# Joining a weight's low word by two 16-bit operations in place of a 32-bit shift and an and-or

## The chip, the core and the metric

One core of one Trainium2 chip runs the whole program as one launch. The metric is the device time of that launch in microseconds (us). It is given as a median of several executions, and one execution was also taken with the hardware profiler. Five engines work from queues of their own: PE (TensorE, matmul), DVE (VectorE), ACT (ScalarE), POOL (GpSimd) and SP (SyncE), which issues most of the DMAs.

## What is computed

Attention over 8 batches of 8 heads, with 32 global rows and 512 local rows per head (a local row sees the global keys and the local keys at most 32 places away), followed by a feed-forward layer on the 4352 rows of 512 features that come out of it:

```python
x = attention(q_l, k_l, v_l, q_g, k_g, v_g)   # (8 * 544, 512)
h = x @ w_in                                  # w_in  (512, 2048)
sp = np.maximum(h, 0.0) + np.log1p(np.exp(-np.abs(h)))
g = h * erf(sp)
out = (g @ w_out).astype(np.float32)          # w_out (2048, 512)
```

The weights arrive as 64-bit floating-point numbers, since setup divides a float32 array by the square root of a NumPy scalar; the kernel gets their bit patterns as 64-bit integers and makes 32-bit numbers of them on the chip.

## The kernel before

**The two stages.** Attention runs head by head. The feed-forward layer runs over nine chunks of rows (eight of 512 and one of the 256 global rows) and in two passes, `ps` 0 and 1, each with one half of the 2048 hidden features. Attention and the first pass are interleaved until some 425 us; after that the first pass ends and the second begins, which goes on until the end. Every matrix product of the feed-forward layer is made of three matmuls on split numbers, high times high, high times low and low times high, in groups that add up in PSUM (names `h` for the first product, `op` for the second, `xh`/`xl`, `gh`/`gl`, `winh`/`winl`, `wouth`/`woutl` for the high and low parts).

**The weights.** They come in sixteen units, four of `w_in` and four of `w_out` for each pass. A unit is one tile `RAW` of 128 partitions by 1024 64-bit words (lines 884 to 930, `load_unit`); two such tiles are in use in turn. Six steps make a high and a low part of it:

- `last_bits`: the lower 32-bit word becomes its own top three bits (DVE).
- `sign`: the sign bit of the upper word is put in with them (DVE).
- `rebase`: the upper word, read as a float32, is multiplied by 2 to the power -112 (ACT or DVE).
- `whole`: the upper word is shifted left by 3 and the lower word is put in (DVE).
- a copy to the high part (ACT or DVE), and a subtraction for the low part (DVE or POOL).

All of the first four work in place. Each of them reads and writes one 32-bit word of every two, so it takes steps of 8 bytes over the 1024 numbers of a partition:

```python
def word(n):
    return RAW.ap.bitcast(I32).rearrange("p (n two) -> p n two", two=2)[:, :, n]
```

Eight units are made between 16 and 128 us (first pass) and eight between 430 and 546 us (second pass). The second pass also makes sums and differences of weight parts (`sums`, line 1016: tiles `sx`, `sy`, `s0h` to `s3l`), which lie in buffers that the weights of the first pass had (line 1019). `s3l` takes the buffer `oh2`, and so comes after the last matmul that reads `wouth` of unit 2 of the first pass.

**The order.** No engine chooses at run time. `Program.schedule` (line 147) goes through all operations with a cost for each, such as `{"DVE": 0.67}` for `last_bits` and `{"DVE": 1.16}` for `sign`, and writes one fixed order per engine; until some 54 us it also puts matmuls on a constant (tile `spare`) where PE would otherwise have nothing. The engines then run their lists in order and wait for each other by semaphores. Lines 350 to 373 hold the helpers that record every instruction, so most instructions of PE have line 350, those of ACT line 352, and those of DVE and POOL line 371.

Of the kernel before, what the change touches and what calls it, by code (L numbers as in the profile page):

```python
# [13 lines left out]
BF16 = mybir.dt.bfloat16  # L14
I32 = mybir.dt.int32
I64 = mybir.dt.int64
AF = mybir.ActivationFunctionType
ALU = mybir.AluOpType
AX = mybir.AxisListType
# [48 lines left out]
SET_EXP = "exp_and_others"  # L68
SET_SOFTPLUS = "softplus"
SET_ERF = "sigmoid_and_others"  # L70


def s32(v):
    return v - (1 << 32) if v >= 1 << 31 else v


def win_start(b):
# [22 lines left out]
class Program:  # L100
# [9 lines left out]
    def add(self, ways, key, fn, reads=(), writes=(), moved=0.0, heat=0, issues=1, fetch=0, mode=0):  # L110


        op = Op()
        op.ways, op.fn, op.key, op.seq, op.moved = ways, fn, key, len(self.ops), moved
        op.heat, op.issues, op.fetch, op.mode = heat, issues, fetch, mode
        op.outs, op.at, op.new, op.eng = [], 0.0, [], None
        op.slack = max(SLACK.get(e, 0.0) for e in ways)
        op.port = not any(b.pool in self.psum for b in reads)
        deps = set()
        for b in reads:  # L120
            deps.update(b.writers)
        for b in writes:
            deps.update(b.writers)
            deps.update(b.readers)
            if b not in self.allocated:
                self.allocated.add(b)
                if b.pool is not None:
                    op.new.append(b)
        op.bufs = [b for b in dict.fromkeys([*reads, *writes]) if b.pool is not None]
        for b in op.bufs:  # L130
            b.users += 1
        for b in writes:
            b.writers, b.readers = [op], []
        for b in reads:
            if b not in writes:
                b.readers.append(op)
        op.waits = len(deps)
        for d in deps:
            d.outs.append(op)
        self.ops.append(op)  # L140
        return op
# [170 lines left out]
def kernel(  # L312
# [43 lines left out]
    def dma(*a, **k):  # L356
        i = pinned(nc.sync.dma_start(*a, **k))
        if DEPTH <= len(issued) < FEW:
            after = mybir.DependencyInfo(mybir.DependencyClass.Sync, mybir.DependencyReason.DATA)
            tc.add_manual_dep(i.ins, issued[-DEPTH].ins.name, after, reason="few in flight")  # L360
        issued.append(i)
        return i
# [10 lines left out]
    dve, pool = Pin(nc.vector), Pin(nc.gpsimd)  # L373
    vec = {"DVE": dve, "POOL": pool}

    def copy(e, dst, src):
        if e == "ACT":
            act(dst, src, AF.Copy)
        else:
            dve.tensor_copy(dst, src)  # L380
# [38 lines left out]
    part = [dram.tile([SL, DM], F32, name=f"part{c}") for c in range(NCHT)]  # L419
# [25 lines left out]
    def attention(b, h, key):  # L445
# [68 lines left out]
        def exps(src, k):  # L514
            for t in range(4):
                act(SM.ap[:, t, :], src[:, t, :], AF.Exp, bias=MX.ap[:, t : t + 1], scale=k)

        def scaled_exps():
            act(MX.ap, MX.ap, AF.Copy, scale=-scale)
            exps(S.ap, scale)  # L520
# [10 lines left out]
        else:  # L531
# [7 lines left out]
            )  # L539
            add({"ACT": 0.55}, key, lambda: act(SM.ap, SM.ap, AF.Exp, scale=scale), [TAB], [SM])  # L540
        if b * H + h < TURN:
# [52 lines left out]
    def weighted_end(b, h, nm, key, O, XN):  # L594
# [11 lines left out]
        def norm(e):  # L606
# [4 lines left out]
            else:  # L611
                for t in range(4):
                    act(XN.ap[:, t, r0 : r0 + D], O.ap[:, t, :D], AF.Copy, scale=RS.ap[:, t, :])

# [97 lines left out]
    def half_keys(key, nm, qks, GA, GB):  # L712
# [30 lines left out]
        def exps():  # L743
            for r, T in enumerate((GA, GB)):
                src = T.ap[:, :384].rearrange("p (m x) -> p m x", x=P)
                dst = PG.ap[:, 3 * r : 3 * r + 3, :]
                for x in (slice(0, WB), slice(2 * WB, 4 * WB)):
                    act(dst[:, :, x], src[:, :, x], AF.Exp, bias=NM.ap[:, r : r + 1], scale=scale)

# [131 lines left out]
    def mbuf(shape, dtype, name, tag, bufs):  # L881
        return Buf(mp, shape, dtype, name, tag, bufs)

    def load_unit(kind, src, half, u, hi, lo, key, deps=()):
        HI, LO = (
            Buf(pool, [P, 2, 512], F32R, f"w{kind}{x}_{half}_{u}", tag)
            for x, (pool, tag) in (("h", hi), ("l", lo))
        )
        RAW = mbuf([P, 1024], I64, f"raw_{kind}_{half}_{u}", "raw", 2)

        def fetch():
            for i in range(2):
                dma(RAW.ap[:, 512 * i : 512 * i + 512], src[half, u][:, 512 * i : 512 * i + 512])

        add({"SP": 0.9}, key - RLEAD, fetch, deps, [RAW, HI, LO], moved=1048.0, issues=2)

        def word(n):
            return RAW.ap.bitcast(I32).rearrange("p (n two) -> p n two", two=2)[:, :, n]

        def last_bits():  # L900
            dve.tensor_scalar(word(0), word(0), 29, None, op0=ALU.logical_shift_right)

        def sign():
            dve.scalar_tensor_tensor(word(0), word(1), s32(0x80000000), word(0), op0=ALU.bitwise_and, op1=ALU.bitwise_or)

        def rebase(e):
            w = word(1).bitcast(F32)
            if e == "ACT":
                act(w, w, AF.Copy, scale=REBASE)
            else:  # L910
                dve.tensor_scalar(w, w, REBASE, None, op0=ALU.mult)

        def whole():
            dve.scalar_tensor_tensor(word(1), word(1), 3, word(0), op0=ALU.logical_shift_left, op1=ALU.bitwise_or)

        flat = lambda t: t.ap.rearrange("p a n -> p (a n)")
        LOW, UP = Buf(None, None, None, None, None), Buf(None, None, None, None, None)
        add({"DVE": 0.67}, key, last_bits, [RAW], [LOW])
        add({"DVE": 1.16}, key, sign, [RAW, LOW], [LOW, UP])
        add({"ACT": 1.05, "DVE": 0.67}, key, rebase, [RAW, UP], [UP])  # L920
        add({"DVE": 1.16}, key, whole, [RAW, LOW, UP], [UP])
        add({"ACT": 1.05, "DVE": 0.67}, key, lambda e: copy(e, flat(HI), word(1).bitcast(F32)), [RAW, UP], [HI])
        add(
            {"POOL": 2.45, "DVE": 1.16},
            key,
            lambda e: vec[e].tensor_tensor(flat(LO), word(1).bitcast(F32), flat(HI).bitcast(F32), ALU.subtract),
            [RAW, HI, UP],
            [LO],
        )
        W[kind, half, u] = (HI, LO)  # L930
# [363 lines left out]
    for u in range(NU):  # L1294
        load_unit("in", w_in, 0, u, (wpool, f"ih{u}"), (wpool, f"il{u}"), WIN[u])
        load_unit("out", w_out, 0, u, (wpool, f"oh{u}"), (wpool, f"ol{u}"), WOUT[u])
# [9 lines left out]
    def load_late(i):  # L1306
        kind, src, u = ("in", w_in, i) if i < NU else ("out", w_out, i - NU)
        load_unit(kind, src, 1, u, late[2 * i], late[2 * i + 1], LATE[i], [ATTN])
# [8 lines left out]
    for ps in range(2):  # L1317
        for c in ORDER[ps]:
            n = NV if c < B else NU
# [110 lines left out]
```

## Time and profile before

| | us |
|---|---|
| median of 3 executions | 904.11 |
| lowest and highest of them | 901.39, 904.65 |
| the profiled execution, its own time | 905.85 |
| the profiled execution, span from the first to the last instruction | 904.04 |
| busy in the span: PE, DVE, ACT, POOL | 891.8, 674.5, 522.2, 244.2 |

The span is 1.81 us shorter than the profiled execution's own time. [...] A busy share is an average over the whole span; the stages differ, and PE's instructions are pipelined, so a short hole between two matmuls can be read better from their starts than from the idle time that is given for them.

### The profile page before, as it was taken

Reading aid. Unit: us, or ns where it says so; the run is one execution under the profiler, and the core shown is the slowest. Engines: PE = TensorE matmul, PEld = TensorE weight load, DVE = VectorE, ACT = ScalarE, POOL = GpSimd, SP = SyncE. Lnnn points to the kernel's source line nnn. Section 1 sums busy time; section 2 is a strip of 40 time slices with the busy share of each in tenths; the row PEclk is TensorE's granted clock in tenths of the full one; section 3 lists DMA queues with packets and bytes.
Section 4 is the critical chain, followed back from the end, with each engine's and each line's share of the span. In section 5 each row is a group of like instructions: output and inputs, shape, how many; then the busy total and the mean of one; then the engine's idle time right before and its main releaser. Section 6 shows DMA issues by size and latency. Waiting matters only on the chain.

```text
span 904.0 us, 22910 instructions
## 1 busy us (share of the span) xinstructions
PE 891.8 (99%) x9289; PEld 736.2 (81%) x9300; DVE 674.5 (75%) x1567; ACT 522.2 (58%) x962; POOL 244.2 (27%) x181
## 2 busy tenths in 40 slices
PE   9999999999999999999999999999999999999998
PEld 5677777777777777778898888988999899999986
DVE  3899797667757676773985898898878787787553
ACT  4778882855557466663756664655454545453540
POOL 0002242312533115330510324354222323233100
PEclk9999999999999999999999999999999999999999
DMA  9997988889798898975452210321324152303034
GB/s 349 349 314 232 301 256 241 303 242 319 261 257 276 252 307 269 278 239 164 131 136 95 115 47 1 71 63 33 70 71 94 57 115 60 96 24 95 1 94 116
DMA packets 93209, 153.53 MB, mean 170 GB/s; under 512 B 11952, under 2 KB 55728, under 8 KB 93104
## 3 DMA queue, kind: packets, MB, share of 16 engines
q1 hardware_dynamic: 92912, 151.81, 53.9%
q8 instruction: 73, 1.20, 0.6%
q10 hardware_dynamic: 192, 0.26, 0.1%
q14 instruction: 32, 0.26, 0.1%
HBM read 111.41 MB, written 40.63 MB: 168 GB/s over the span
## 4 chain that ended last, share of the span: by engine, by line
PE 80%; DVE 12%; DMA 4%; issue 2%; ACT 1%; POOL 1%; SPq 0%; DVEq 0%; POOLq 0%
PE op L350 34%; PE h L350 32%; PE s L350 5%; DVE raw_in L371 2%; PE o L350 2%; PE spare L350 2%; PE ga L350 2%; DMA rx<-xsc 2%; DVE xl L371 2%; DVE hs L371 1%; PE go L350 1%; PE s L351 1%; DVE gl L371 1%; DVE xh L371 1%; DVE sp L371 1%
## 5 line engine op out<-in xcount | busy, mean ns | idle before, releaser
L350 PE MATMUL op<-wouth,gh 128*128 128x512 f32 x544 | 217.5, 400 | 0.6 <-issue 0.6
L350 PE MATMUL op<-woutl,gh 128*128 128x512 f32 x544 | 212.4, 390 | 0.0
L350 PE MATMUL op<-wouth,gl 128*128 128x512 f32 x544 | 212.1, 390 | 0.0
L371 POOL TENSOR_TENSOR sp<-sp,hs 128x512 f32<-128x512 f32 x78 | 113.0, 1471 | 271.6 <-ACT sp L352 271.6
L350 PE MATMUL h<-xh,winh 128*128 128x512 f32 (+1 forms) x464 | 164.6, 355 | 0.6 <-DVE hs L371 0.5
L350 PE MATMUL h<-xh,winl 128*128 128x512 f32 (+1 forms) x464 | 162.2, 350 | 0.0
L350 PE MATMUL h<-xl,winh 128*128 128x512 f32 (+1 forms) x464 | 162.0, 349 | 0.0
L350 PEld LDWEIGHTS op<-wouth,gh 128*128 128x128 f32 x544 | 102.2, 188 | 27.3 <-issue 6.4
L350 PEld LDWEIGHTS op<-wouth,gl 128*128 128x128 f32 x544 | 102.1, 188 | 22.2
L350 PEld LDWEIGHTS op<-woutl,gh 128*128 128x128 f32 x544 | 102.3, 188 | 19.0 <-issue 0.5
L353 ACT ACT_TABLE_LOAD x90 | 115.5, 1283 | 2.3 <-PEq L1417 0.7
L352 ACT ACTIVATE gh<-sp 128x512 fp32r<-128x512 f32 x85 | 52.0, 631 | 92.8 <-PE op L350 84.4
L371 DVE TENSOR_TENSOR gl<-sp,gh 128x512 fp32r<-128x512 f32 x105 | 96.5, 939 | 7.2 <-ACT gh L352 6.4
L350 PEld LDWEIGHTS h<-xh,winh 128*128 128x128 f32 x464 | 87.7, 189 | 17.1 <-issue 2.7
L352 ACT ACTIVATE hs<-h 128x512 f32<-128x512 f32 (+1 forms) x68 | 36.9, 543 | 110.4 <-PE h L350 110.0
L350 PEld LDWEIGHTS h<-xl,winh 128*128 128x128 f32 x464 | 87.8, 189 | 12.0
L350 PEld LDWEIGHTS h<-xh,winl 128*128 128x128 f32 x464 | 87.7, 189 | 11.7
L371 DVE TENSOR_TENSOR hs<-h,hs 128x256 f32<-128x256 f32 x196 | 76.5, 417 | 11.8 <-PE h L350 7.7
L352 ACT ACTIVATE sp<-hs 128x512 f32<-128x512 f32 x136 | 74.9, 620 | 0.7 <-DVE gl L371 0.4
L352 ACT ACTIVATE sp<-sp 128x512 f32<-128x512 f32 x136 | 74.8, 620 | 0.4
L371 POOL TENSOR_TENSOR gl<-sp,gh 128x512 fp32r<-128x512 f32 x31 | 46.4, 1505 | 80.2 <-ACT gh L352 41.9
L371 DVE CAST gh<-sp 128x512 fp32r<-128x512 f32 x51 | 32.9, 652 | 43.2 <-PE op L350 42.8
(179 smaller groups left out, 1538.9 us busy)
## 6 DMA issues: line engine op xcount, KB each, us to landing
vb<-in_vB_dram SPq DMA_DIRECT2D x32, 650.0 KB, 5.7
qk<-in_qk_dram SPq DMA_DIRECT2D x30, 656.0 KB, 7.0
rx<-xsc SPq DMA_DIRECT2D x52, 256.0 KB, 5.2
va<-in_vA_dram SPq DMA_DIRECT2D x32, 390.0 KB, 5.8
px<-tp SPq DMA_DIRECT2D x84, 128.0 KB, 4.8
pt<-px SPq DMA_DIRECT2D x21, 512.0 KB, 5.5
raw_in<-in_w_in_dram SPq DMA_DIRECT2D x16, 512.0 KB, 7.3
xsc<-xT SPq DMA_DIRECT2D x32, 256.0 KB, 5.5
```

Of the source, the lines that this page charges most:

```text
L350: pe = lambda n, *a, **k: pinned(nc.tensor.matmul(n, *a, **k))
L351: tr = lambda *a, **k: pinned(nc.tensor.transpose(*a, **k))
L352: act = lambda *a, **k: pinned(nc.scalar.activation(*a, **k))
L353: table = lambda name: pinned(nc.scalar.preload_act_table_set(name))
L371: return lambda *a, **k: pinned(f(*a, **k))
```

## The change

`sign` no longer joins two tensors. `last_bits` shifts the upper 16 bits of the lower word right by 13 and writes the result to that word's lower 16 bits. `sign` then takes the sign bit out of the upper word's top 16 bits and writes it, alone, over the lower word's upper 16 bits. Together the two halves are the word that stood there before. Both operations have one tensor as input, a constant, and 16-bit elements in steps of 8 bytes, 1024 of them per partition.

```diff
+U16 = mybir.dt.uint16
...
-def s32(v):
-    return v - (1 << 32) if v >= 1 << 31 else v
...
+        def part(n):
+            return RAW.ap.bitcast(U16).rearrange("p (n four) -> p n four", four=4)[:, :, n]
+
         def last_bits():
-            dve.tensor_scalar(word(0), word(0), 29, None, op0=ALU.logical_shift_right)
+            dve.tensor_scalar(part(0), part(1), 13, None, op0=ALU.logical_shift_right)
 
         def sign():
-            dve.scalar_tensor_tensor(word(0), word(1), s32(0x80000000), word(0), op0=ALU.bitwise_and, op1=ALU.bitwise_or)
+            dve.tensor_scalar(part(1), part(3), 0x8000, None, op0=ALU.bitwise_and)
```

The costs that the planner is given stay as they were (0.67 and 1.16), so the five lists stay too: in the built programs the order of instructions on every engine is the same, with the same waits, but for sixteen places on DVE where a SCALAR_TENSOR_TENSOR on a tile `raw_in` or `raw_out` has become a TENSOR_SCALAR. Line numbers of the functions that follow are lower by 3, and by 0 to 3 in `load_unit` itself.

## Rows read from the trace of the kernel before

**Rows 1.** The page: busy time, share of the span and instructions of each engine.
```profile
PE 891.8 (99%) x9289; PEld 736.2 (81%) x9300; DVE 674.5 (75%) x1567; ACT 522.2 (58%) x962; POOL 244.2 (27%) x181
```
**Rows 2.** Busy time by stretch; columns as the first line names them.
```profile
core 0: us, PE busy (x) PEld busy (x) DVE busy (x) ACT busy (x) POOL busy (x), PEclk, DMA share, GB/s
17.00:30.00 13.00, 12.15 (x244) 8.76 (x235) 12.85 (x27) 10.76 (x29) 0.00 (x0) 1.00 1.02 409
38.00:80.00 42.00, 41.20 (x864) 31.16 (x866) 40.88 (x85) 34.39 (x97) 0.75 (x1) 1.00 0.85 286
...
620.00:800.00 180.00, 180.00 (x1135) 163.66 (x1135) 145.49 (x280) 90.73 (x154) 59.74 (x42) 1.00 0.29 71
```
**Rows 3.** What PE waited for: total us, times, longest.
```profile
PE h L350 <- DVE hs L371: 0.8, 3, 0.3
...
PE h L350 <- DVE x L371: 0.5, 1, 0.5
PE ga L350 <- DVE winl L371: 0.5, 1, 0.5
```
**Rows 4.** The chain that ended last, 27 to 38 us: start, us, what.
```profile
29.72 0.45 issue
30.18 0.55 PE ga L350 x24
...
35.99 0.45 issue
```
**Rows 5.** DVE's groups by shape: busy us, mean ns | idle before.
```profile
L371 DVE SCALAR_TENSOR_TENSOR raw_in<-raw_in 128x1024 int32<-128x1024 int32 x16 | 20.8, 1302 | 0.3
...
L371 DVE CAST xh<-xT 128x512 fp32r<-128x512 f32 x4 | 1.7, 426 | 0.2 <-ACT xT L352 0.2
```
**Rows 6.** Tile raw_out's instructions: duration ns min/median/max, first and last start.
```profile
L371 DVE SCALAR_TENSOR_TENSOR raw_out<-raw_out x16: 1216/1226/2002, 46.8 to 540.7; 128x1024 int32<-128x1024 int32 x16
L371 DVE TENSOR_SCALAR raw_out<-raw_out x12: 673/693/1100, 46.1 to 538.9; 128x1024 int32<-128x1024 int32 x8, 128x1024 f32<-128x1024 f32 x4
```
**Rows 7.** DVE in order of time, 429 to 460 us: start, us, instruction.
```profile
448.09 1.78 DVE L371 TENSOR_SCALAR raw_in<-raw_in 128x1024 int32<-128x1024 int32 x1
449.91 1.23 DVE L371 SCALAR_TENSOR_TENSOR raw_in<-raw_in 128x1024 int32<-128x1024 int32 x1
...
456.08 1.22 DVE L371 SCALAR_TENSOR_TENSOR raw_out<-raw_out 128x1024 int32<-128x1024 int32 x1
```
**Rows 8.** PE in order of time, 458 to 459 us.
```profile
458.16 0.28 PE L350 MATMUL h<-xl,winh 128*128 128x256 f32 x1
458.28 0.28 PE L350 MATMUL h<-xh,winl 128*128 128x256 f32 x1
458.68 0.39 PE L350 MATMUL h<-xh,winh 128*128 128x256 f32 x1
```
**Rows 9.** DVE, then POOL, in order of time, 520 to 550 us.
```profile
522.61 1.23 DVE L371 SCALAR_TENSOR_TENSOR raw_in<-raw_in 128x1024 int32<-128x1024 int32 x1
...
537.20 1.22 DVE L371 SCALAR_TENSOR_TENSOR raw_out<-raw_out 128x1024 int32<-128x1024 int32 x1
...
545.28 1.78 DVE L371 TENSOR_TENSOR s3l<-sy,s3h 128x512 fp32r<-128x512 f32 x1
...
544.66 1.85 POOL L371 TENSOR_TENSOR sp<-sp,hs 128x512 f32<-128x512 f32 x1 [3.06 <-ACT sp L352]
547.20 1.61 POOL L371 TENSOR_TENSOR sy<-winl,winl 128x512 f32<-128x512 f32 x1 [0.69 <-DVE s3l L371]
```
**Rows 10.** PE in order of time, around 545 and 567 to 570 us.
```profile
544.70 0.39 PE L350 MATMUL op<-wouth,gl 128*128 128x512 f32 x1
...
566.84 0.28 PE L350 MATMUL h<-x,winh 128*128 128x256 f32 x1
567.65 0.39 PE L350 MATMUL h<-x,winh 128*128 128x256 f32 x1 [0.53 <-DVE x L371]
...
570.18 0.39 PE L350 MATMUL h<-xh,winh 128*128 128x256 f32 x1 [0.24 <-DVE hs L371]
```

## The prediction

> **What bounds the kernel now.** I read the busy time by engine first. PE is busy for 99% of the span, DVE for 75% [rows 1]. A saving on DVE is therefore worth only what it takes out of PE's holes, and the next question is where PE has holes that DVE makes. The table by stretch shows the end of the program: from 620 to 800 us PE is busy for 180.00 of 180 us [rows 2], so whatever is gained before 620 us is kept to the end, and nothing can be gained there. The list of PE's waits names DVE seldom: three short waits on `hs`, one on `x` and one on `winl`, 1.8 us together [rows 3], and one each on `mx` and `xl` at places where no weight is made. The list rests on modelled ends of matmuls, so I measure a hole from start to start of two matmuls.
>
> Of the first five, three matter. At 458.68 us a matmul starts 0.40 us after the one before it, where its neighbours are 0.12 us apart [rows 8]: a hole of 0.28 us, in a stretch where DVE makes four weight units in a row. At 567.65 us the distance is 0.81 us [rows 10]: a hole of 0.69 us before `x`. At 570.18 us there is another, 0.24 us by the profile. The one on `winl` at 30.18 us I don't count: the named instruction ended 0.45 us before PE went on, and 6 us later PE stops for the same 0.45 us with nobody named [rows 4]. That looks like a stop of PE's own. The other waits on `hs` lie behind 600 us, when no weight is made any more.
>
> **The change, term by term.** Two operations of each unit change, so sixteen of each. Four things decide.
>
> *The price of `sign`.* Today it is one of 32 SCALAR_TENSOR_TENSORs (sixteen `sign`, sixteen `whole`), with a median of 1.226 us for 1024 numbers [rows 5, 6], which is about 1.2 ns per number. It becomes a TENSOR_SCALAR. The one-tensor operations on the same tile, with the same steps of 8 bytes, take 0.693 us [rows 6], nearly half. No row has a 16-bit operation, so I bound it. Below: the shortest row for one tensor is 0.426 us for 512 numbers [rows 5]; if 16-bit numbers went twice as fast as 32-bit ones, 1024 of them would take that. Above: the present 1.226 us, one number at a time. I take 0.693 us, because that row is nearest in operation, tile, count and step, and only the width of the element differs. The gain is 1.226 - 0.693 = 0.533 us per unit.
>
> *The price of `last_bits`.* The same bounds, and the same value: 0.693 us, so no change.
>
> *The sum on DVE.* 16 x 0.533 = 8.5 us less busy time, eight units before 130 us and eight after 430 us.
>
> *What of it reaches PE.* In the first 130 us I count nothing. DVE is full there, 12.85 of 13 us and 40.88 of 42 us, but so is PE, 12.15 of 13 and 41.20 of 42 [rows 2], with a list fixed beforehand that includes idle matmuls on `spare`; a datum that is ready sooner moves none of them. In the second pass, four units are made before the hole at 458.68 us. Part of their lead is lost on the way: `last_bits` at 448.09 us took 1.78 us instead of 0.69 because a POOL operation held it up [rows 7], and an instruction that arrives there sooner only waits longer. Behind it, the `sign` operations at 449.91 and 456.08 us [rows 7] still give 2 x 0.533 = 1.07 us, more than the hole. It closes: 0.28 us gained, hidden by nothing, and then PE itself is late next. Before `x` at 567.65 us two more `sign` operations, at 522.61 and 537.20 us, bring DVE ahead by 1.07 us, but `s3l` at 545.28 us must wait for the last matmul on the buffer that it takes over. That matmul started at 544.70 and took 0.39 us [rows 9, 10], so it ended at 545.09, only 0.19 us before `s3l` began. With the 0.28 us that PE is then ahead, `s3l` can start 0.47 us sooner, and POOL's sums, which follow it [rows 9], and `x` with them. PE resumes 0.47 us sooner, of which 0.28 it had already. The hole at 570.18 us ends on DVE too and moves along.
>
> Sum: 0.28 + 0.19 = 0.47 us. The profiled execution took 905.85 us, which makes 905.4; it stood 0.2% above the median of 904.11, against which I forecast **903.6 us**. The ends of this sum are 0 (the lead is lost at POOL's operations each time) and 0.28 + 0.69 + 0.24 = 1.21 us (no lead is lost). About 0.5%, or 4.5 us, is what a measurement of this kernel can tell from no change; the three executions lie 3.3 us apart.
>
> [...] The int32 row takes one word of every two at 0.693 us for 1024, that is 0.68 ns per number [rows 6], so a step of two words costs nothing that can be seen. [...]
>
> **The rivals.**
>
> *The 16-bit parts go slowly (slower).* Elements narrower than a word may lose the faster rate, so that both operations take 1.226 us as a two-tensor operation does. `sign` then gains nothing and `last_bits` costs 1.226 - 0.693 = 0.533 us more per unit. For it: the trace has no 16-bit operation on DVE. Against it: the one-tensor rows keep their rate with a step, and the instruction stays of the same kind. Six units of the second pass lie ahead of the two holes with no cover left, 6 x 0.533 = 3.2 us on PE. In the first pass DVE is full in the two stretches, which hold seven of the eight units: between 0 and 3.7 us, so I put in the middle, 1.9. Together 5.1 us, 909.2. It decides against the change once the pair takes about 0.5 us more than today's 0.693 + 1.226 = 1.92 us. [...]
>
> *The lead is not lost (faster, though not by 0.5%).* `s3l` finds its buffer free, or the 16-bit operations take 0.426 us each, which saves another 0.53 us per unit. Then all three holes close, 1.21 us, and in the first pass some of the two units at 17 to 30 us may show, 1.07 us at most: 2.3 us, 901.8.
>
> *DVE bounds the first 130 us after all (faster).* The stretch from 38 to 80 us, with DVE at 40.88 of 42, speaks for it; PE's 41.20 and the empty list of waits there against it. Every one of the eight units would then shift PE by 0.533 us, 4.3 us, and with the holes 5.5 us: 898.6.
>
> *Nothing arrives.* POOL's operations hold DVE up after every lead, or `sign` stays at 1.2 us because the rate hangs on something else than the count of tensors. Then the time is 904.1.
>
> **How the numbers follow.** Forecast 0.65, lead not lost 0.12, nothing arrives 0.10, slow parts 0.09, DVE bounds the start 0.04. The first three stay within 0.5%: same 0.87; slower 0.09; faster 0.04. The likeliest cases run from 901.8 to 904.1 us by their sums; medians of this kernel scatter by one or two us around that, as the three executions show. So the range is 900.5 to 906.2 us; it leaves out the two outer cases, which hold 0.13.
>
> **What would show it right or wrong.** In the profile after, the sixteen `sign` operations stand as TENSOR_SCALARs on 16-bit parts at about 0.69 us, and `last_bits` stays at 0.69; DVE's busy time falls from 674.5 to about 666 us. The hole at 458.68 us is gone; the one before `x` is still there, shortened by some 0.2 us. PE's busy time stays, and 620 to 800 us is as full as before. The forecast is wrong if either operation takes 1.2 us or more, which I would see at once in the groups by shape, or if the first `op` matmuls at 131 us start more than 1 us earlier or later, which would mean that the first pass does hang on DVE.

## The result, and the profile after

The changed kernel took **910.04 us** (median of 11 executions, 905.81 to 911.74) beside 903.53 us (901.39 to 905.11, 11) for the kernel before. The ratio is 1.0066, with a 95% interval of 1.0049 to 1.0084. On another chip, later, it was 910.40 beside 903.45 us, ratio 1.0068 (1.0048 to 1.0089). So the change costs some 6 to 7 us, over the 0.5% that can be told from no change. The prediction was 903.6 us with a range of 900.5 to 906.2; the time lies outside it, on the side of the rival "The 16-bit parts go slowly".

The profiled execution took 910.59 us with a span of 908.8, 4.8 us longer than the span before. Busy time by engine, on the page of the changed kernel, answering to [rows 1]:

```profile
PE 893.3 (98%) x9300; PEld 737.1 (81%) x9300; DVE 688.4 (76%) x1567; ACT 522.4 (57%) x962; POOL 245.7 (27%) x181
```

DVE was to fall from 674.5 to 666 us; it rose to 688.4. The instructions on the tiles `raw_in` and `raw_out` say why (duration in ns min/median/max, then first and last start, then the shapes), beside [rows 6]:

```profile
L368 DVE TENSOR_SCALAR raw_in<-raw_in x21: 696/1332/2424, 16.6 to 527.8; 128x1024 uint16<-128x1024 uint16 x16, 128x1024 f32<-128x1024 f32 x5
...
L368 DVE TENSOR_SCALAR raw_out<-raw_out x20: 684/1323/1833, 47.2 to 543.5; 128x1024 uint16<-128x1024 uint16 x16, 128x1024 f32<-128x1024 f32 x4
L368 DVE SCALAR_TENSOR_TENSOR raw_out<-raw_out x8: 1197/1224/2004, 51.9 to 545.3; 128x1024 int32<-128x1024 int32 x8
```

Most of these instructions are the 16-bit ones, so the medians are theirs: 1.32 and 1.33 us. Singly they read 1.30 to 1.36 us where nothing holds them up. Both parts of the pair cost that, so a pair takes about 2.65 us in place of 0.693 + 1.226 = 1.92: **0.73 us more per unit**, of which `last_bits` makes 0.63 and `sign` 0.10. The longer ones, up to 2.42 us, stood beside POOL's work (that one, at 435.07 us, beside 5.71 us of it from 432.77), as the one of 1.78 us did before (beside 2.10 us of POOL's work from 447.23) [rows 7].

Where it reaches PE, the list of PE's waits shows (total us, times, longest), beside [rows 3]:

```profile
PE h L347 <- DVE hs L368: 2.6, 4, 1.9
PE h L347 <- DVE xl L368: 1.3, 3, 0.6
PE s L347 <- DVE pt L368: 1.1, 1, 1.1
PE ga L347 <- DVE winl L368: 1.0, 1, 1.0
...
PE h L347 <- DVE x L368: 0.8, 1, 0.8
```

The wait on `hs` that lasts 1.9 us is the hole of 458.68 us, grown. PE of the changed kernel in order of time, beside [rows 8]:

```profile
458.12 0.28 PE L347 MATMUL h<-xh,winl 128*128 128x256 f32 x1
460.35 0.39 PE L347 MATMUL h<-xh,winh 128*128 128x256 f32 x1 [1.95 <-DVE hs L368]
...
461.29 0.41 PE L347 MATMUL h<-xl,winh 128*128 128x256 f32 x1
461.50 0.41 PE L347 MATMUL h<-xh,winl 128*128 128x256 f32 x1
461.72 0.41 PE L347 MATMUL h<-xh,winh 128*128 128x256 f32 x1
```

And DVE's list that leads there, the copy to `hs` ahead of the four units, then the end of the fourth unit and the copy that PE waits for; the two copies of the kernel before come first:

```profile
429.79 0.69 DVE L371 COPY hs<-h 128x512 f32<-128x512 f32 x1 [5.07 <-PE h L350]
...
457.94 0.68 DVE L371 COPY hs<-h 128x512 f32<-128x512 f32 x1
```
```profile
428.77 0.69 DVE L368 COPY hs<-h 128x512 f32<-128x512 f32 x1 [5.06 <-PE h L347]
...
455.37 1.35 DVE L368 TENSOR_SCALAR raw_out<-raw_out 128x1024 uint16<-128x1024 uint16 x1
456.50 1.25 DVE L368 TENSOR_TENSOR winl<-raw_in,winh 128x1024 fp32r<-128x1024 f32 x1
457.67 2.03 DVE L368 TENSOR_SCALAR raw_out<-raw_out 128x1024 uint16<-128x1024 uint16 x2
459.62 0.68 DVE L368 COPY hs<-h 128x512 f32<-128x512 f32 x1
```

(The row with x2 is `sign` and the `rebase` behind it.) Ahead of the four units DVE stood 1.02 us earlier than before; behind them it stands 1.68 later. It has lost 2.70 us, nearly the 4 x 0.73 = 2.92 that the price gives. The copy is queued behind the fourth unit's `sign`; PE needs the buffer that it empties, and stops for 2.23 - 0.12 = 2.11 us.

Then PE does something that no row of before showed: it runs slower. From 461.29 us its matmuls of 256 columns stand 0.21 us apart instead of 0.12. The windows of the changed kernel (stretch, length, then the engines' busy time; the granted clock is the third number from the end):

```profile
425.00:460.00 35.00, 32.78 (x161) 27.53 (x159) 30.80 (x26) 26.41 (x40) 12.02 (x7) 1.00 0.57 178
460.00:461.00 1.00, 0.65 (x5) 0.65 (x6) 1.00 (x2) 0.00 (x0) 0.00 (x0) 1.00 1.14 214
461.00:462.00 1.00, 1.00 (x8) 1.00 (x8) 1.00 (x3) 0.54 (x1) 0.00 (x0) 0.64 0.92 307
462.00:463.00 1.00, 1.00 (x7) 1.00 (x6) 1.00 (x4) 1.00 (x2) 0.28 (x1) 0.50 1.00 401
463.00:464.00 1.00, 1.00 (x6) 1.00 (x6) 1.00 (x1) 0.68 (x2) 1.00 (x1) 0.50 0.36 143
464.00:465.00 1.00, 1.00 (x8) 1.00 (x7) 1.00 (x1) 0.00 (x0) 1.00 (x1) 0.66 0.00 0
465.00:470.00 5.00, 5.00 (x29) 4.35 (x29) 5.00 (x7) 1.72 (x3) 1.69 (x2) 1.00 0.01 3
```

The granted clock reads 0.64 in the first microsecond from 461 us on, 0.50 in the next two, 0.66 in the fourth and 1.00 from 465 us on. Sixteen distances, from 461.29 us on, take 3.41 us there instead of 16 x 0.12 = 1.92, so 1.5 us are lost on top of the stop. Before, the clock was 1.00 in these stretches:

```profile
425.00:460.00 35.00, 34.88 (x176) 29.62 (x176) 29.85 (x28) 26.74 (x41) 11.41 (x7) 1.00 0.65 192
460.00:465.00 5.00, 5.00 (x37) 4.66 (x36) 4.66 (x4) 3.12 (x6) 3.89 (x2) 1.00 0.51 181
```

Short holes follow, one where `xl` comes late, two where `x` does, and one with nobody named (PE again, beside [rows 10]; two rows of the kernel before come first):

```profile
564.80 0.28 PE L350 MATMUL h<-xl,s1h 128*128 128x256 f32 x1
...
578.70 0.28 PE L350 MATMUL h<-xh,s3h 128*128 128x256 f32 x1
```
```profile
568.49 0.39 PE L347 MATMUL h<-xl,s1h 128*128 128x256 f32 x1 [0.37 <-DVE xl L368]
...
571.03 0.38 PE L347 MATMUL h<-x,winh 128*128 128x256 f32 x1 [0.25 <-ACT x L349]
572.17 0.39 PE L347 MATMUL h<-x,winh 128*128 128x256 f32 x1 [0.76 <-DVE x L368]
...
583.42 0.39 PE L347 MATMUL h<-xh,s3h 128*128 128x256 f32 x1
```

The matmuls at 568.49 and 583.42 us stood 3.69 and 4.72 us earlier before, at 564.80 and 578.70. So the account of this execution: PE 1.67 us behind at 460.35, some 3.2 behind at 465, 3.7 and 4.7 at these two rows, and 4.8 at the end of the span. The last hole, at 583.42, may not be the change's: `nosign` below, with less work on DVE, has one at the same matmul.

### The profile page after: what moved, and what is told of

Same layout as the page of the kernel before. It is cut to its first block, busy times and chain, and to the rows that moved or that the text cites. A ratio compares the mean times of both kernels' runs of the same rounds, so it can differ in the third digit from the quotient of the medians.

```text
span 908.8 us, 22921 instructions
## 1 busy us (share of the span) xinstructions
PE 893.3 (98%) x9300; PEld 737.1 (81%) x9300; DVE 688.4 (76%) x1567; ACT 522.4 (57%) x962; POOL 245.7 (27%) x181
## 4 chain that ended last, share of the span: by engine, by line
PE 73%; DVE 16%; DMA 4%; issue 3%; ACT 1%; POOL 1%; SPq 1%; DVEq 0%; POOLq 0%
PE op L347 32%; PE h L347 30%; PE s L347 4%; DVE raw_in L368 3%; DMA px<-tp 3%; DVE raw_out L368 2%; PE o L347 2%; DVE xl L368 2%; PE spare L347 1%; DVE hs L368 1%; PE ga L347 1%; SPq L354 1%; DVE xh L368 1%; PE go L347 1%; DVE gl L368 1%
## 5 line engine op out<-in xcount | busy, mean ns | idle before, releaser
L368 POOL TENSOR_TENSOR sp<-sp,hs 128x512 f32<-128x512 f32 x78 | 115.7, 1505 | 270.4 <-ACT sp L349 257.4
L347 PEld LDWEIGHTS h<-xh,winl 128*128 128x128 f32 x464 | 88.4, 191 | 11.7
```

The lines of the kernel that those rows point to most:

```text
L347: pe = lambda n, *a, **k: pinned(nc.tensor.matmul(n, *a, **k))
L368: return lambda *a, **k: pinned(f(*a, **k))
```

## The experiments

Each group ran on one chip, beside executions of the kernel before on the same chip; ratios are to those. A ratio is not the quotient of the two medians beside it and can differ from that by up to 0.2%; losses in per cent are read from the ratios.

### The price of one operation, by itself

`probe` is a small kernel of its own that runs single DVE operations, four times each. Its tiles, with the shape of the operation (`shift` is a shift right by 13; the others at the same places are a product, `mbf16step`, a copy, `ncopy16step`, and two-tensor and-ors, `k16two` with 16 bits every 8 bytes and `o32two` with 32):

```
a16step   shift(part(a, 4, 0), part(a, 4, 1))       16 bits, every 8 bytes, as in the change
b32step   shift(word(a, 2, 0), word(a, 2, 0))       32 bits, every 8 bytes, as before
c16step   shift(a.bitcast(U16), a.bitcast(U16))     16 bits, dense
d16step   shift(part(a, 2, 0), part(a, 2, 1))       16 bits, every 4 bytes
e16thick  shift(a.bitcast(U16), part(wide, 4, 1))   16 bits, read every 8 bytes, written dense
f16thin   shift(part(a, 4, 0), thin.bitcast(U16))   16 bits, read dense, written every 8 bytes
i32step   shift(a, a)                               32 bits, dense
j32step   shift(word(a, 4, 0), word(a, 4, 0))       32 bits, every 16 bytes
```

> This kernel computes nothing of the reference (its output is zeros); it runs single DVE operations on 1024 numbers per partition, four times each, first alone and then (tiles with a q) beside POOL's products on 512 floats. In the changed kernel a 16-bit part of an 8-byte weight takes 1.30 to 1.37 us where a 32-bit word of it takes 0.69. Theory W (the width and the step together lose a rate): the 16-bit operation at a step of 4 takes about 1.33 us alone as well, the dense 16-bit one 0.43 to 0.69, the 32-bit word at a step of 2 takes 0.69. Theory N (narrow numbers are slow in any arrangement): the dense 16-bit one takes 1.3 too. Theory L (it is the kernel's load, POOL or the DMAs, that slows them): alone they take 0.69, and 1.3 only beside POOL. The operations that read thick and write dense, or read dense and write thin, tell whether the read or the write is to blame: if the write (two bytes inside a word), only the second is slow; if the read, only the first. A 32-bit word at a step of 4 (16 bytes): 0.69 if the step costs nothing, 1.3 or more if it does. The two-tensor 16-bit operation: 1.23 as for words, or about 1.3.

The groups by line and shape (busy us, mean ns | idle before), 1024 numbers per partition each; names without their last number, `q` marks the series beside POOL:

```profile
L30 POOL TENSOR_TENSOR grind<-grind 128x512 f32<-128x512 f32 x40 | 57.7, 1443 | 83.4 <-DVE grind L30 80.3
...
L30 DVE SCALAR_TENSOR_TENSOR k16two<-k16two 128x1024 uint16<-128x1024 uint16 x4 | 9.7, 2422 | 0.1
...
L30 DVE TENSOR_SCALAR a16step4q<-a16step4q 128x1024 uint16<-128x1024 uint16 x4 | 7.1, 1772 | 0.1
...
L30 DVE TENSOR_SCALAR b32step2q<-b32step2q 128x1024 int32<-128x1024 int32 x4 | 5.7, 1422 | 0.1
...
L30 DVE TENSOR_SCALAR f16thin<-dense 128x1024 uint16<-128x1024 uint16 x4 | 5.2, 1302 | 0.1
L30 DVE TENSOR_SCALAR mbf16step<-mbf16step 128x1024 bf16<-128x1024 bf16 x4 | 5.2, 1301 | 0.1
L30 DVE COPY ncopy16step<-ncopy16step 128x1024 uint16<-128x1024 uint16 x4 | 5.2, 1300 | 0.1
L30 DVE TENSOR_SCALAR a16step<-a16step 128x1024 uint16<-128x1024 uint16 x4 | 5.2, 1299 | 0.1
...
L30 DVE SCALAR_TENSOR_TENSOR o32two<-o32two 128x1024 int32<-128x1024 int32 x4 | 4.9, 1226 | 0.1
L30 DVE TENSOR_SCALAR j32step<-j32step 128x1024 int32<-128x1024 int32 x4 | 4.3, 1073 | 0.1
...
L30 DVE TENSOR_SCALAR d16step<-d16step 128x1024 uint16<-128x1024 uint16 x4 | 2.9, 736 | 0.1
L30 DVE TENSOR_SCALAR b32step<-b32step 128x1024 int32<-128x1024 int32 x4 | 2.8, 696 | 0.1
L30 DVE TENSOR_SCALAR e16thick<-src 128x1024 uint16<-128x1024 uint16 x4 | 2.8, 694 | 0.1
L30 DVE TENSOR_SCALAR i32step<-i32step 128x1024 int32<-128x1024 int32 x4 | 2.8, 694 | 0.1
...
L30 DVE TENSOR_SCALAR c16step<-c16step 128x1024 uint16<-128x1024 uint16 x4 | 1.7, 427 | 0.1
```

The operation costs 1.299 us alone, so it isn't the kernel's load (theory L falls), and dense 16-bit numbers take 0.427, less than dense 32-bit ones at 0.694, so narrow numbers aren't slow as such (theory N falls). It is the **write**: reading every fourth part and writing dense takes 0.694, reading dense and writing every fourth 1.302. At a step of 4 bytes the operation takes 0.736. A shift, a copy and a bfloat16 product at the places of the change cost the same (1.299, 1.300 and 1.301). Two tensors at that step take 2.422 us, twice the 1.226 of 32-bit words; there reads and write were not taken apart. Whether the width of the number decides, or the step counted in numbers, these rows leave open: at a step of two numbers both widths are near the 0.694 of dense 32-bit numbers (0.736 and 0.696), at a step of four both take longer (1.302 and, for 32 bits every 16 bytes, 1.073, with read and write not taken apart). Beside POOL's products the operation takes 1.772 against 1.299 alone, and the 32-bit shift of before 1.422 against 0.696, so both are held up there.

### Which pass, and is it plain time

`first` is the changed kernel with this, and the same in `sign`; `second` has `half == 1` instead:

```diff
-            dve.tensor_scalar(part(0), part(1), 13, None, op0=ALU.logical_shift_right)
+            if half == 0:
+                dve.tensor_scalar(part(0), part(1), 13, None, op0=ALU.logical_shift_right)
+            else:
+                dve.tensor_scalar(word(0), word(0), 29, None, op0=ALU.logical_shift_right)
```

`extra` is the kernel before with one line more in `last_bits`:

```diff
             dve.tensor_scalar(word(0), word(0), 29, None, op0=ALU.logical_shift_right)
+            dve.tensor_scalar(word(0), word(0), 0, None, op0=ALU.bitwise_or)
```

> Only the eight units of the first pass (up to 130 us) have the 16-bit operations. Theory A (the first pass has room, as the trace of the changed kernel shows PE level with before at 453 us): 903.5 us, within 1.5. Rival B (each of the seven units in which DVE is full shifts PE, 0.73 us each, and something later hides it in the trace): about 3 to 5 us more, 907 to 908.

> Only the eight units of the second pass (430 to 540 us) have the 16-bit operations. Theory A: the whole loss is here, 908 to 910 us, with the hole before the matmul at 460 us at about 2 us and a granted clock below 1.00 just behind it. Rival B: half of the loss, 905 to 907 us.

> The kernel before with one more one-tensor 32-bit operation in each unit (bits or-ed with 0, 0.69 us by the rows of before), and no 16-bit operation. Theory A (it is the plain time on DVE that arrives, whatever operation takes it): the same as the changed kernel within 2 us, 907 to 911, with the same hole at 460 us and the fall of the granted clock behind it. Rival C (something of the 16-bit operations besides their time, the way they hold POOL up or are held up): 905.5 us or less, with no fall of the clock.

Beside 904.43 us for the kernel before: `first` 905.36 us, ratio 1.0017 (1.0003 to 1.0031); `second` 909.48, 1.0057 (1.0040 to 1.0075); `extra` 912.10, 1.0071 (1.0047 to 1.0095). The second pass makes most of the loss. The first pass has room for most of its 8 x 0.73 = 5.8 us of longer operations, not for all: by the ratio some 1.5 us arrive (0.3 to 2.8), more than theory A allows and less than rival B asks. Two places are seen in its trace, PE's waits on `xT` and on `pt`:

```profile
24.78 0.38 PE L347 MATMUL s<-mask 128*128 128x512 bf16 x1 [0.39 <-ACT xT L349]
...
79.23 0.24 PE L347 MATMUL s<-va,pt 128*32 128x65 f32 x1 [1.06 <-DVE pt L368]
```

Both waits stand in the two traces of the changed kernel, in `first` and in `extra`, and in none of the ten other traces that have the order of before. PE's wait on `winl` near 30 us, 1.06 us in `first` instead of 0.50 [rows 3], is no such place: `second_again` below, with the first pass of before, has 0.88 us there.

`extra` has no 16-bit operation, as much busy time on DVE as the changed kernel, and the same loss and hole (its median lies 1.1 us over the 911 that was expected at most, its ratio within the changed kernel's interval). The page's first line, then PE around the hole:

```profile
PE 891.0 (98%) x9300; PEld 735.2 (81%) x9300; DVE 687.8 (76%) x1583; ACT 521.8 (58%) x962; POOL 246.1 (27%) x181
```
```profile
456.92 0.28 PE L347 MATMUL h<-xh,winl 128*128 128x256 f32 x1
...
459.21 0.39 PE L347 MATMUL h<-xh,winh 128*128 128x256 f32 x1 [2.01 <-DVE hs L368]
```

So theory A holds: it is plain time on DVE. In this execution the clock did not fall behind the hole, against what was expected of it: the hole alone doesn't decide that.

### Each operation, and what a cheaper one would bring

`signonly` leaves `last_bits` as it was before. `nosign` leaves the step `sign` out altogether. `signonly`, against the changed kernel:

```diff
-            dve.tensor_scalar(part(0), part(1), 13, None, op0=ALU.logical_shift_right)
+            dve.tensor_scalar(word(0), word(0), 29, None, op0=ALU.logical_shift_right)
```

`nosign`, against the kernel before:

```diff
-            dve.scalar_tensor_tensor(word(0), word(1), s32(0x80000000), word(0), op0=ALU.bitwise_and, op1=ALU.bitwise_or)
+            pass
```

`dense16` gives the pair of the second pass a tile of its own, where each number has 4 bytes:

```diff
+        JOIN = Buf(wb_pool, [P, 1024], I32, f"join_{half}_{u}", "join", 2) if half else Buf(None, None, None, None, None)
...
+                dve.tensor_scalar(low_part(0), part(1), 13, None, op0=ALU.logical_shift_right)
...
+                dve.tensor_scalar(low_part(1), part(3), 0x8000, None, op0=ALU.bitwise_and)
...
-            dve.scalar_tensor_tensor(word(1), word(1), 3, word(0), op0=ALU.logical_shift_left, op1=ALU.bitwise_or)
+            dve.scalar_tensor_tensor(word(1), word(1), 3, low(), op0=ALU.logical_shift_left, op1=ALU.bitwise_or)
```

> Only the sign step is a 16-bit operation, the last bits stay a 32-bit shift at 0.69 us. By the durations of the changed kernel the sign step then costs 1.30 to 1.37 us in place of 1.23, so 0.1 us per unit. Theory A (plain time on DVE): before plus 0 to 1.5 us, 904 to 906, so that nearly all of the change's loss is that of the last bits. Rival: half of the loss or more, 907 and over, if it is the 16-bit write beside the other users of the tile that costs.

> The eight units of the second pass alone: the two 16-bit operations write into a tile of their own with 4 bytes per number (the step of the writes is 4 bytes instead of 8), and the step that joins the words reads the lower word from there. The first pass is as before. By the operations measured alone (0.736 us at a step of 4 bytes) the pair takes 1.47 us instead of 1.92, 0.45 us less per unit. Theory A: they take 0.69 to 0.74 each, the hole at 458.68 us closes, and the time is that of before less 0.3 to 1.2 us, 903.2 to 904.1 beside 904.4. Rival 1: reading one part of four costs too, and they stay at 1.3: as in the run with the change in the second pass alone, 908 to 910. Rival 2: they take 0.74, but nothing arrives: the same as before within 0.3.

> The sign step is left out (the weights lose their sign), all else is as before, so 1.23 us less DVE time per unit, 16 units. It bounds what any cheaper sign step could bring. Theory A (PE has three short holes that DVE makes, 1.2 us together, and the first pass has room): 0.3 to 1.5 us less than before, 903 to 904. Rival B (DVE bounds the first pass): 3 us less or more, 901.5 or below. If losses arrive in full (0.7 us per unit cost some 5 us) and gains hardly, the kernel stands at the edge: PE is full, and only DVE time on top of its slack counts.

Beside 904.20 us: `signonly` 903.55 us, ratio 1.0010 (0.9996 to 1.0023); `dense16` 904.16, 1.0006 (0.9989 to 1.0024); `nosign` 903.12, 0.9989 (0.9974 to 1.0004). None can be told from no change. So nearly all of the loss is, by subtraction, that of `last_bits`, the half of the change that the prediction took to cost nothing (a kernel with `last_bits` alone was not run). And no saving in `sign` can pay here: with the step gone, 1.23 us per unit, the most that the interval allows is 0.26%. The trace of `nosign` shows why, DVE and then PE at the place of the hole:

```profile
457.82 0.69 DVE L368 COPY hs<-h 128x512 f32<-128x512 f32 x1 [2.43 <-PE h L347]
```
```profile
458.58 0.28 PE L347 MATMUL h<-xh,winl 128*128 128x256 f32 x1
458.70 0.28 PE L347 MATMUL h<-xh,winh 128*128 128x256 f32 x1
```

The hole is closed, as forecast (0.12 us between the two matmuls), and then DVE waits 2.43 us for PE. A lead beyond 0.28 us is waited away. Before `x` the distance is 0.60 us (567.12 to 567.72 us) instead of 0.81 [rows 10], which is the 0.2 us that the prediction expected of a lead there. In `dense16` the operations of the pair take 0.764 and 0.762 us by their medians (rival 1 falls):

```profile
L368 DVE TENSOR_SCALAR join<-raw_in x8: 735/764/1855, 431.9 to 523.7; 128x1024 uint16<-128x1024 uint16 x8
L368 DVE TENSOR_SCALAR join<-raw_out x8: 745/762/772, 454.6 to 537.8; 128x1024 uint16<-128x1024 uint16 x8
```

The hole is closed there too, the distance before `x` is 0.61 us, and DVE's copy waits 0.79 us for PE, but no gain can be measured; theory A's 0.3 to 1.2 us and rival 2 can't be told apart by this interval. It is the change with cheap writes, and it beats nothing: no version run here is faster than the kernel before.

### Which units, and a new plan

`early4` has the change only in the four units ahead of the copy to `hs`, by a condition like that of `first`; `late4` only in the four later ones of the second pass, `("out", 1), ("out", 2), ("in", 1), ("out", 3)`:

```diff
+        late_unit = half == 1 and (kind, u) in (("in", 3), ("in", 2), ("in", 0), ("out", 0))
```

`replan` tells the planner the new costs, on its own scale:
```diff
-        add({"DVE": 0.67}, key, last_bits, [RAW], [LOW])
-        add({"DVE": 1.16}, key, sign, [RAW, LOW], [LOW, UP])
+        add({"DVE": 1.27}, key, last_bits, [RAW], [LOW])
+        add({"DVE": 1.27}, key, sign, [RAW, LOW], [LOW, UP])
```

> Only the four units of the second pass that stand on DVE ahead of the copy to hs at 458 us (w_in units 3, 2 and 0, w_out unit 0) have the 16-bit operations. Theory A (PE waits for that copy, which is queued behind them): 0.73 us per unit, less what is lost where DVE waits for POOL, so a hole of about 2 us before the matmul at 460 us and, where the granted clock falls behind it, 1.4 us more: before plus 1.5 to 4 us, 905.7 to 908 beside 904.2. Rival (the four later units make the loss): the same as before.

> Only the four later units of the second pass (w_out units 1 and 2, w_in unit 1, w_out unit 3, 498 to 546 us) have the 16-bit operations. Theory A: no hole at 460 us and no fall of the clock; the three small waits between 564 and 579 us grow by what the changed kernel shows there, 1.8 us: before plus 0.5 to 2.5 us, 904.7 to 906.7. Rival 1 (the early four make all of it): the same as before. Rival 2: these make most of it, 907 or more.

> The changed kernel, with the planner told what the two operations cost on this scale (1.27 and 1.27 us in place of 0.67 and 1.16), so that it makes new lists for all engines. If the loss is only that the copy to hs stands behind operations that are longer than planned, a new order can take much of it back: 904 to 908. If the lists of before are better for another reason, or DVE has no room, 909 and over.

Beside 904.87 us: `early4` 906.37, 1.0016 (1.0000 to 1.0032); `late4` 906.58, 1.0008 (0.9992 to 1.0025); `replan` 931.20, 1.0295 (1.0258 to 1.0331). This new plan takes nothing back: all five lists change, and in its trace PE waits for `hs` twice, 7.1 us the longer time. The lists of before are worth more here than costs nearer to the measured ones; other plans were not tried.

The two halves came to about 2 us, where `second` had cost 5 on another chip. So both, the whole second pass and the changed kernel ran once more, on one chip:

> The changed kernel once more, beside its parts on one chip. If the chip decides whether TensorE's granted clock falls behind the hole at 460 us, the share of executions with a mean clock below 0.999 (8 of 11 so far in this kernel or near it) is another here, and the time with it: 910 where it falls, 907 to 908 where it does not. If the fall belongs to the kernel, 908.5 to 911 beside 904.

> The eight units of the second pass with the 16-bit operations, as before, on the same chip as its two halves. Theory A (the parts add up, and chips differ): the sum of the two halves' losses within 1.5 us, some 906 to 908. Rival (the two halves together bring down the clock where each alone does not): 909 and over, with the clock below 0.999 in most executions, while the halves stay at 905 to 906.5.

> The four early units alone, on the same chip as the whole: 1.5 to 3 us over before. If the clock falls behind the hole at 460 us on this chip, then here too, since the later units come behind that place: as often as in the run with all eight.

> The four later units alone, on the same chip as the whole: 0.5 to 1.8 us over before, and no execution with the clock below 0.999.

Beside 903.45 us: `after_again` 910.40, 1.0068 (1.0048 to 1.0089); `second_again` 908.75, 1.0053 (1.0032 to 1.0073); `early4_again` 908.21, 1.0050 (1.0031 to 1.0068), over the 3 us that were expected at most; `late4_again` 904.54, 1.0014 (1.0000 to 1.0027). Here the parts add up within their intervals: 0.50% + 0.14% beside 0.53%. PE at the hole, `early4_again` and then `late4_again`:

```profile
457.50 0.28 PE L347 MATMUL h<-xh,winl 128*128 128x256 f32 x1
459.73 0.39 PE L347 MATMUL h<-xh,winh 128*128 128x256 f32 x1 [1.95 <-DVE hs L368]
```
```profile
457.94 0.28 PE L347 MATMUL h<-xh,winl 128*128 128x256 f32 x1
458.30 0.39 PE L347 MATMUL h<-xh,winh 128*128 128x256 f32 x1
```

The four early units make the hole and most of the loss. Their loss differs between the two chips (0.16% and 0.50%, intervals that hardly overlap), but the hole does not: 2.21 us from start to start in the trace of `early4`, 2.23 in that of `early4_again`, with the clock at 1.00 behind both. The mean clock over the execution was 0.998 or less in 4 of 6 executions of `early4_again`, and in 1 of 12 of `early4`. In the changed kernel it was so in 9 of 17, with a median of 910.6 us against 908.2 in the other 8. The difference of 2.4 us is of the order of the 1.5 us read from the rows above. But the clock does not explain the chips: `second` had such a mean in 8 of 9 executions and `second_again` in 1 of 7, and they lost 0.57% and 0.53%; the two executions of `early4_again` without it took 907.1 and 907.9 us, some 4 us over before as well. What decides whether the clock falls behind a hole of 2 us stays open, and so does what made `early4_again` lose some 4.5 us, where the grown hole (2.11 - 0.28 = 1.83 us) and the clock (1.5 us) account for 3.3 at most.

## Why the prediction was wrong

- **The step that failed** is "*The price of `last_bits`.* The same bounds, and the same value: 0.693 us, so no change." It measured 1.30 to 1.36 us. The reason given under `sign`, "that row is nearest in operation, tile, count and step, and only the width of the element differs", left out what decides: a 2-byte write every 8 bytes runs at about half the rate of a 4-byte write every 8 bytes (1.302 against 0.696 us). The step was the same only in bytes; counted in numbers it was four instead of two. No row of before had a narrow write, and I let four likenesses outweigh the one difference.
- **The upper bound** of 1.226 us was too low as well, by 0.07 to 0.13 us. "One number at a time" was my estimate of the slowest case; no run shows how many numbers DVE takes at a time.
- **The price of `sign`**: 0.693 forecast, 1.30 to 1.36 measured, so +0.10 us per unit instead of -0.533. That would have been harmless, as `signonly` shows.
- **The sum on DVE**: -8.5 us forecast, +13.9 found; 16 x 0.73 = 11.7 of it are the price.
- **What of it reaches PE.** The mechanism was right. The hole at 458.68 us closes when DVE is ahead and hangs on it when DVE is late; the hole before `x` shortens by the 0.2 us that were forecast for a lead (`nosign` and `dense16`). But the forecast asked only how a lead is lost, and a lead and a delay count differently: PE has 0.28 us to give there, and a delay has no end.
- **The first 130 us** were counted as nothing; some 1.5 us arrive, near the rival's middle of 1.9. The reason, that a datum that is ready sooner moves none of PE's matmuls, speaks of a lead and not of a delay. Leaving out PE's stop near 30 us was right. The sign that was named for this stage does not decide: the first `op` matmuls start at 131.88 and 130.78 us in the changed kernel's two traces and at 132.56 in `first`, beside 130.3 to 131.1 in the kernels with the first pass of before.
- **The rival "The 16-bit parts go slowly"** was right in kind and nearly in time, 909.2 us, in part by luck. Its 0.533 us per unit should be 0.73, and it lacked the clock, which makes it too low; and it let the time of six units reach PE whole, which makes it too high: 6 x 0.73 = 4.4 us of price came to some 3.2 us of grown holes (1.83 at `hs`, 1.4 at `xl` and `x`), as much as its own 6 x 0.533 = 3.2. It got a chance of 0.09 because the rows with a step kept their rate. They were 32-bit rows, and the text said that no row has a 16-bit operation: that called for more than 0.09.

## What to carry to other kernels

Count what an instruction writes, not only how many tensors it reads: here a one-tensor operation on 1024 16-bit parts took 0.694 us where they were read every 8 bytes and written dense, 0.736 where they were read and written every 4 bytes, and 1.302 where they were read dense and written every 8. When PE is full, price an edit on another engine for a delay first: the saving was cut off here by the next wait for PE (2.43 us in `nosign`), the delay was not, once the slack of 0.28 us at that place was used up (a stop of 2.11 us), and in the changed kernel's profiled execution a granted clock of 0.50 behind the stop cost 1.5 us on top. If an edit has two halves, and one of them "costs nothing" by likeness to another row, that half needs a bound of its own and a chance to match.

## What the runs showed that I had not expected

- A write of 2 bytes every 8 nearly halves DVE's rate for one tensor: 1.302 us against 0.696 for 4 bytes every 8. With two tensors read and one written at that step it is 2.422 against 1.226. Why this is so, no run here shows.
- 32-bit words every 16 bytes take 1.073 us where every 8 bytes take 0.696.
- After a stop of 2 us in a stretch where PE had been full, the granted clock went down to 0.50 in the changed kernel's profiled execution and PE ran slower for 3.41 us; it stayed at 1.00 in those of `extra`, `early4` and `early4_again`, with 2.29, 2.21 and 2.23 us from start to start.
- One kernel lost different amounts on two chips: the four early units 0.16% on one and 0.50% on the other, while the changed kernel lost 0.66% and 0.68%.
